# Row-paired transposes of the rows and of the attention output through the output's PSUM bank, and xT ahead of weighting

## The chip, the core and the metric

The kernel runs on one core of a Trainium2 chip. A core has TensorE (PE in the profile; PEld is its loading of weights), VectorE (DVE), ScalarE (ACT), GpSimd (POOL) and SyncE (SP, which here only starts transfers). PSUM, where TensorE writes, has eight banks. The metric is the device time in microseconds of one execution, as the median over several runs; lower is better.

## What is computed

Four layers follow one another: attention with a memory, a gated feed-forward layer, and both once more, each with a layer norm in front and a residual addition behind. Cut to what matters, the reference is:

```python
# x: 2048 x 448; 16 heads of 256; memory of 8 rows; segments of 32 rows
for s in range(64):
    h = concatenate([mem, x[32*s:32*s+32]])        # 40 rows of 448
    q, k, v = h @ Wq, h @ Wk, h @ Wv               # for each head
    p = softmax(mask(q @ k.T * scale))             # 40 x 40 for each head
    o = sum over heads of (p @ v) @ Wo
    mem = o[:8]                                    # goes on to the next segment
    outs.append(o[8:])
...
x = x + attention(layernorm(x))
x = x + (relu(g) * u) @ W_down                     # g, u = layernorm(x) @ W_gate, @ W_up
x = x + attention(layernorm(x))                    # the same weights again
x = x + (relu(g) * u) @ W_down
```

The memory makes the segments of an attention layer a recurrence of 64 steps.

## The kernel before

**Tiling and stages.** Ahead of the loop the weights are combined: Wq with Wk to A_sb (with its last 64 input dimensions in A3 and A3z), Wv with Wo to B_sb, so that scores are (h A) h^T and outputs are sums of (p h) B. Then the loop `for g in range(nsteps + 1)` calls `step(g, ff)`. Two chains run in one step: chain 0 is the first attention layer at segment g, chain 1 the second one at segment g - 4. The steps with g below 4 or above 63 have one chain. The 40 rows of each chain lie transposed in `hT` (dimensions on partitions, four chunks of 128 columns, chain 0 in columns 0 to 39, chain 1 in columns 64 to 103 of each). Every other step, from g = 3, also carries a `Feed` (ff): the residual of the attention output, layer norm, both feed-forward layers for 128 rows, and the rows for later segments. These steps are called fed here, the others bare. One more Feed closes the kernel.

**The order of work.** `mm` and `tr` hang each TensorE instruction on the one before it (`in_order`), so TensorE's order is the order of the program. The other engines' queues are ordered by the framework's planner; VectorE's and ScalarE's order may differ from the program's. Where `keep_in_program_order` stands (the layer norm, the loads ahead of the loop), the order holds there too. An engine's queue runs strictly in turn.

**PSUM.** The pool has seven banks under the tag "ps", handed out in turn, and one bank under the tag "ox", which `step` takes at its start (L592) and fills in `project_out` up to `finish`.

**One step, as far as the change touches it** (`step`, from L745):
- b0, b2: two banks of half 0's projection are opened (`open_banks`, with 64-row matmuls, two row groups side by side: the last 64 input dimensions) and closed (`close_bank`, 128-row matmuls, then copied out to TQ). A bank of index 4 (z0, z1) is copied out to TZ in two parts, one on VectorE, one on ScalarE.
- In a fed step `ff.residual()` (L404): four transposes of the attention output OT into the tile otp, and one VectorE addition to the rows `xa`; then `row_stats`.
- b1, b3, z0, z1 are opened, z0, b1, b3 closed. `hk_make` (L597) transposes the rows hT into the tile kps with four transposes; VectorE copies all of it to hk, ScalarE a second form of the last chunk. z1 is closed.
- c0, c2, c1, c3 (half 1's banks) are opened; `scores_m(0)` makes the memory's scores Sm of half 0, and VectorE and ScalarE their weights PM; c0, c2, c1, c3 are closed, with `ff.norm()` in between.
- With both chains: `flipped(PM[0])` transposes PM to pps, VectorE copies it to PT; `scores_x(0)` makes Sx; `weigh_m(0)` (L630) makes ya and yb from hk and PT, copied into Y or Z; `ff.xposed()` (L414) transposes the normed rows xn to tps and copies them to xT, once on VectorE, twice on ScalarE; then `scores_m(1)`, `scores_x(1)`, and the weights of half 0.
- `project_out(0, 0, 10)` multiplies Y or Z with B_sb into ox; the Feed's `gate_up` (ups, gps from xT) follows. `flipped_rows` (L566) transposes the later weights in pairs of row groups, into two banks ppr.

Of the kernel before, what the change touches and what calls it, by code (L numbers as in the profile page):

```python
# [8 lines left out]
BF = mybir.dt.bfloat16  # L9
F32 = mybir.dt.float32  # L10
I32 = mybir.dt.int32
AF = mybir.ActivationFunctionType
ALU = mybir.AluOpType
AX = mybir.AxisListType

DM = 448
# [5 lines left out]
L = MEM + SEG  # L22
# [9 lines left out]
HI = 128  # L32
HW = 5 * HI
W = 2 * L
# [6 lines left out]
ROWS = (slice(0, 64), slice(64, 128))  # L41
# [12 lines left out]
def build_kernel(ctx, tc, A_x, A_mem0, A_Wq, A_Wk, A_Wv, A_Wo, B_W_gate, B_W_up, B_W_down, out,  # L54
                 ntiles=16, nseg=64):
    nc = tc.nc
    P = nc.NUM_PARTITIONS
# [10 lines left out]
    psum = ctx.enter_context(tc.tile_pool(name="psum", bufs=7, space=bass.MemoryType.PSUM))  # L68
# [4 lines left out]
    def in_order(r):  # L73
        if last_pe[0] is not None:
            tc.add_manual_dep(r.ins, last_pe[0],
                              mybir.DependencyInfo(mybir.DependencyClass.NoSync,
                                                   mybir.DependencyReason.DATA),
                              reason="order of issue")
        last_pe[0] = r.ins.name

    def mm(*a, **k):
        in_order(nc.tensor.matmul(*a, **k))  # L82

    def tr(*a):
        in_order(nc.tensor.transpose(*a))  # L85

    def evac(eng, dst, src):
        if eng is nc.scalar:
            nc.scalar.copy(dst, src)  # L89
        else:  # L90
            eng.tensor_copy(dst, src)  # L91
# [10 lines left out]
    ident = glob.tile([P, P], BF, name="ident")  # L102
# [50 lines left out]
    for hf in range(2):  # L153
        t = glob.tile([P, 5, 6, 64], BF, name=f"TQ{hf}")
        nc.gpsimd.memset(t[:], 0.0)
        TQ.append(t)

    def row_stats(t):

        stats = p_ln.tile([P, nc.vector.BN_STATS_DIM], F32, tag="ln_stats")  # L160
        nc.vector.bn_stats(stats[:], t[:])
        mv = p_ln.tile([P, 2], F32, tag="ln_mv")
        nc.vector.bn_aggr(mv[:], stats[:])
        rstd = p_ln.tile([P, 1], F32, tag="ln_rstd")
        nc.gpsimd.tensor_scalar(out=rstd[:], in0=mv[:, 1:2], scalar1=EPS, scalar2=None, op0=ALU.add)
        nc.gpsimd.tensor_tensor(out=rstd[:], in0=rstd[:], in1=half[:], op=ALU.pow)
        return t, mv, rstd
# [213 lines left out]
    OT = main.tile([P, 4, 128], BF, name="OT")  # L381
# [11 lines left out]
    class Feed:  # L393
# [8 lines left out]
            self.nx = xp[i % 2]  # L402

        def residual(self):  # L404
            tp = psum.tile([P, 4, 128], BF, tag="ps", name="otp")
            for kd in range(4):
                tr(tp[:, kd, :], OT[:, kd, :], ident[:])
            nc.vector.tensor_tensor(self.x[:], tp[:].rearrange("p k d -> p (k d)")[:, 0:DM], self.x[:], op=ALU.add)
            self.st = row_stats(self.x)

        def norm(self):
# [54 lines left out]
    def moving(hb, j, idx, chains, rows=slice(0, P)):  # L466

        if len(chains) == 2:
            return hb[rows, j, idx * HI:(idx + 1) * HI].rearrange("p (c k) -> p c k", k=64)[:, :, 0:L]
        c = chains[0]  # L470
        return hb[rows, j, idx * HI + 64 * c:idx * HI + 64 * c + L]
# [34 lines left out]
    def close_bank(bk, chains, hb, j, eng):  # L506

        n = L * len(chains)
        hf, N = bk.hf, len(bk.tiles)
        for t in bk.tiles:  # L510
            for kd in range(3):
                mm(bk.out(t, n), A_sb[:, kd, hf, t, :], moving(hb, j, kd, chains), start=False, stop=(kd == 2),
                   skip_group_check=True)
        ps = bk.ps
        if bk.i < 4:
            at = 2 * (bk.i // 2) + bk.i % 2
            parts = [(eng, slice(0, P), TQ[hf][:].rearrange("p g (k b) w -> p g k (b w)", b=2)[:, :, :, 32 * at:32 * at + 32], 3)]
        else:
            parts = [(nc.vector, slice(0, 64), TZ[hf][0:64, :, 0:64].unsqueeze(2), 1),
                     (nc.scalar, slice(64, 128), TZ[hf][0:64, :, 64:128].unsqueeze(2), 1)]  # L520
        for eng, rows, T, K in parts:
            T = T.rearrange("p g k (t q) -> p k t g q", q=16)
            if len(chains) == 2:
                evac(eng, T, ps[rows, 0:N * n].rearrange("p (k t g q) -> p k t g q", k=K, t=N // K, q=16))
                continue
            c = chains[0]
            src = ps[rows, 0:N * n].rearrange("p (k t w) -> p k t w", k=K, t=N // K)
            x, m = (0, SEG) if c == 0 else (MEM, 0)
            evac(eng, T[:, :, :, 2, MEM * c:MEM * c + MEM], src[:, :, :, m:m + MEM])
            evac(eng, T[:, :, :, 3 * c:3 * c + 2, :],  # L530
                 src[:, :, :, x:x + SEG].rearrange("p k t (g q) -> p k t g q", q=16))

    def queries(hf, g, kd):
        return TQ[hf][:, g, 2 * kd:2 * kd + 2, :] if kd < 3 else TZ[hf][:, g, :]
# [44 lines left out]
    def active(g):  # L579
        return [c for c in (0, 1) if 0 <= g - c * LAG < nseg]  # L580
# [3 lines left out]
    def step(g, ff):  # L584
        chains = active(g)
        xs = active(g - 1)
        ms = [c for c in chains if g - c * LAG + 1 < nseg]
        gb, j = divmod(g, BLK)
        hb = hTb[gb % 2]
        cols = [(0, 32) if c == 0 else (48, 80) for c in xs] + [(32, 40) if c == 0 else (40, 48) for c in ms]  # L590
        lo, hi = min(a for a, _ in cols), max(b for _, b in cols)
        ox = psum.tile([P, 3, W], F32, tag="ox", bufs=1, name="ox")  # L592

        def ys(hf, later=0):
            return YY[hf][(g + later) % 2]

        def hk_make():  # L597
            kps = psum.tile([P, 4, 128], BF, tag="ps", name="kps")
            for i in range(4):
                tr(kps[:, i, :], hb[:, j, i * HI:(i + 1) * HI], ident[:])  # L600
            hk = HK[g % 2]
            nc.vector.tensor_copy(hk[:, 0:4, :], kps[:])
            nc.scalar.copy(hk[:].rearrange("p k n -> p (k n)")[:, 512:768].rearrange("p (a b) -> p a b", b=64)[:, 0::3, :],
                           kps[:, 3, :].rearrange("p (a b) -> p a b", b=64))
            return hk

        def scores_m(hf):
            if not ms:
                return
            Sp = psum.tile([P, 2, L], F32, tag="ps", name="Sm")  # L610
            for kd in range(4):
                mm(Sp[:, :, :], queries(hf, 2, kd), moving(hb, j, kd + kd // 3, (0, 1)), start=(kd == 0), stop=(kd == 3))
            weights_of(Sp, 2, PM[hf], blk[:], f"m{hf}")
# [16 lines left out]
        def weigh_m(hf, hk, PT):  # L630
            if not ms:
                return
            ya = psum.tile([P, 256], F32, tag="ps", name="ya")
            for kd in range(2):
                mm(ya[:, kd * 128:kd * 128 + 128], hk[:, kd, :], PT[:], start=True, stop=True)
            nc.vector.tensor_copy(ys(hf)[:, 0:16, M0:M0 + 16], ya[:].rearrange("p (t q) -> p t q", q=16))  # L636
            yb = psum.tile([P, 192], F32, tag="ps", name="yb")
            mm(yb[:, 0:128], hk[:, 2, :], PT[:], start=True, stop=True)
            for eo in range(2):
                mm(yb[:, 128:192], hk[:, 4 + eo, :], PT[:, 64 * eo:64 * eo + 64], start=(eo == 0), stop=(eo == 1))  # L640
            nc.scalar.copy(ys(hf)[:, 16:28, M0:M0 + 16], yb[:].rearrange("p (t q) -> p t q", q=16))
# [46 lines left out]

        def project_out(hf, t0, t1):

            for t in range(t0, t1):
                for mc in range(3):
                    mm(ox[:, mc, lo:hi], B_sb[:, hf, t, mc * 128:(mc + 1) * 128],
                       ys(hf)[:, t, lo:hi], start=(hf == 0 and t == 0 and mc == 0),
                       stop=(hf == 1 and t == NT - 1 and mc == 2), skip_group_check=True)
# [56 lines left out]
        b1, b3, z0, z1 = open_banks(chains, hb, j, (0, 1), (0, 3), (0, 4), (1, 4))  # L752
        close_bank(z0, chains, hb, j, None)
        load_some()
        close_bank(b1, chains, hb, j, nc.vector)
        close_bank(b3, chains, hb, j, nc.scalar)
        hk = hk_make()
        close_bank(z1, chains, hb, j, None)
        c0, c2, c1, c3 = open_banks(chains, hb, j, (1, 0), (1, 2), (1, 1), (1, 3))
        scores_m(0)  # L760
        close_bank(c0, chains, hb, j, nc.scalar)
# [5 lines left out]
        if len(chains) == 2:  # L767
            pm = flipped(PM[0], 1, "m0")
            Sx0 = scores_x(0)
            weigh_m(0, hk, pm)  # L770
            if ff is not None:
                ff.xposed()
            scores_m(1)
            Sx1 = scores_x(1)
            probs_x(0, Sx0)
        else:
            Sx0 = scores_x(0)
            if ff is not None:
                ff.xposed()
            scores_m(1)  # L780
            Sx1 = scores_x(1)
            pm = flipped(PM[0], 1, "m0")
            weigh_m(0, hk, pm)
            probs_x(0, Sx0)
# [27 lines left out]
        pm = flipped(PM[1], 1, "m1")  # L812
# [17 lines left out]
    for g in range(nsteps + 1):  # L830
        if g == LAG - 1:
            set_mem(LAG, mem0T[:].unsqueeze(2), (1,))
        i = (g - 3) // 2
# [68 lines left out]
```

## Time and profile before

| what | value |
|---|---|
| runs | 1599.98, 1600.96, 1604.62 us; median 1600.96 |
| the profiled execution | 1600.11 us, of which the span is 1598.3 us |
| mean granted clock of TensorE | 0.993 |
| chain that ended last | PE 89%, DVE 7%, ACT 1%, POOL 1%, issue 1% |
| steps with transposes kps / otp | 68 x 4 / 34 x 4 transposes |
| hk on VectorE / on ScalarE | 68 x 424 ns / 68 x 266 ns |
| residual addition on VectorE | 34 x 381 ns |
| xT on VectorE / on ScalarE | 34 x 421 ns / 68 x 473 ns |
| DMA in the loop | about 10 GB/s |

In lines of a timeline the columns are the start and the duration in us, the engine, the line of the program, the operation, out<-in by tile names, the shapes, and the number of instructions merged into the line. A matmul's duration in the records is its latency, some 0.2 us; the next one starts long before it ends, so the pace of TensorE is read from the distances between starts. In 40 slices of the span, TensorE is busy at 0.9 and more from the sixth slice on, VectorE at 0.7, ScalarE at 0.4 to 0.5.

### The profile page before, as it was taken

To read this page: it belongs to the slowest core of one execution; us is meant where nothing else is said; L and a number is where in the kernel's file an instruction comes from. 1 tells how busy PE (TensorE), PEld (TensorE's weight loads), DVE (VectorE), ACT (ScalarE), POOL (GpSimd) and SP (SyncE) were. 2 spreads that over 40 slices of the span, in tenths; PEclk is the share of its full clock that TensorE was granted. 3 is DMA by queue.
4 is the path that set the end of the run, shared out by engine and by line. 5 is a ranking of instruction groups with operands and counts; after the bars stand their busy time and mean duration, and the time that the engine had idled before them with its cause. 6 is when DMAs were issued, how large, how long until landed. Compare 5 with 4: busy or idle time off the path is not lost.

```text
span 1598.3 us, 96401 instructions
## 1 busy us (share of the span) xinstructions
PE 1567.8 (98%) x44356; PEld 1439.8 (90%) x44356; DVE 1142.5 (71%) x3859; ACT 762.9 (48%) x2239; POOL 92.9 (6%) x240
## 2 busy tenths in 40 slices
PE   8989999999999999999999999999999999999997
PEld 7678899999999999999999999999999999999886
DVE  6856777777777777777777777777777777777773
ACT  5634445544444445544444445544444445544432
POOL 2110000000000000000000000000000000000000
PEclk9989999999999999999999999999999999999999
DMA  9530000000000000000000000000000000000000
GB/s 257 147 102 8 9 9 4 10 9 10 10 10 9 10 10 4 10 10 9 10 10 10 10 10 4 10 10 10 10 9 9 10 10 4 10 8 7 7 7 6
DMA packets 29461, 33.01 MB, mean 21 GB/s; under 512 B 3320, under 2 KB 28160, under 8 KB 29056
## 3 DMA queue, kind: packets, MB, share of 16 engines
q1 hardware_dynamic: 28992, 26.85, 6.3%
q8 instruction: 346, 5.67, 1.5%
q14 instruction: 59, 0.48, 0.1%
q0 software_dynamic: 64, 0.01, 0.0%
HBM read 23.18 MB, written 1.84 MB: 16 GB/s over the span
## 4 chain that ended last, share of the span: by engine, by line
PE 89%; DVE 7%; ACT 1%; POOL 1%; issue 1%; DMA 0%; POOLq 0%; ACTq 0%; DVEq 0%
PE prj L82 25%; PE ox L82 25%; PE ups L82 10%; PE dps L82 6%; PE o L82 5%; PE y L82 4%; PE Sx L82 2%; PE Sm L82 2%; PE bps L82 1%; PE tpw L85 1%; DVE xn L175 1%; DVE TQ L91 1%; PE aps L82 1%; PE gps L82 1%; PE tps L85 1%; PE pps L85 1%
## 5 line engine op out<-in xcount | busy, mean ns | idle before, releaser
L82 PEld LDWEIGHTS <-B_sb 128*128 128x128 bf16 (+1 forms) x15456 | 495.0, 103 | 27.7 <-issue 19.9
L82 PE MATMUL prj<-hT,A_sb 128*128 128x80 bf16 (+1 forms) x11424 | 441.7, 200 | 0.4 <-issue 0.4
L82 PEld LDWEIGHTS <-A_sb 128*128 128x128 bf16 x11424 | 411.9, 100 | 8.9 <-issue 0.5
L82 PE MATMUL ox<-Y,B_sb 128*128 128x80 bf16 (+4 forms) x5880 | 223.0, 198 | 1.8 <-DVE Y L636 1.8
L82 PE MATMUL ox<-Z,B_sb 128*128 128x80 bf16 (+2 forms) x5712 | 217.7, 199 | 1.3 <-DVE Z L636 1.3
L89 ACT CAST TQ<-prj 128x480 bf16<-128x480 f32 (+1 forms) x380 | 178.5, 497 | 83.0 <-PE prj L82 58.7
L82 PE MATMUL gps<-xT,Wgu_sb 64*128 64x128 bf16 (+1 forms) x3332 | 191.3, 214 | 0.8 <-issue 0.5
L82 PE MATMUL ups<-xT,Wgu_sb 64*128 64x128 bf16 (+1 forms) x3332 | 191.1, 214 | 1.0 <-DVE xT L416 0.5
L82 PEld LDWEIGHTS <-Wgu_sb 64*128 64x128 bf16 x6664 | 179.4, 95 | 4.8 <-issue 2.5
L91 DVE CAST TQ<-prj 128x480 bf16<-128x480 f32 (+1 forms) x228 | 129.3, 573 | 13.4 <-PE prj L82 11.2
L432 DVE SCALAR_TENSOR_TENSOR hh<-gps,ut 128x256 bf16<-128x256 f32 (+1 forms) x238 | 95.3, 407 | 48.0 <-ACT ut L431 35.3
L431 ACT CAST ut<-ups 128x256 bf16<-128x256 f32 (+1 forms) x238 | 85.4, 359 | 83.4 <-PE gps L82 64.9
L91 DVE CAST Y<-y 64x128 bf16<-64x128 f32 (+2 forms) x256 | 102.2, 420 | 14.4 <-ACT Y L89 4.5
L89 ACT CAST Y<-y 64x128 bf16<-64x128 f32 (+2 forms) x256 | 89.4, 379 | 46.6 <-DVE Y L91 41.5
L91 DVE CAST Z<-y 64x128 bf16<-64x128 f32 (+2 forms) x256 | 99.2, 418 | 12.4 <-ACT Z L89 5.5
L89 ACT COPY hT<-tps 128x256 bf16<-128x256 bf16 x32 | 11.9, 372 | 197.5 <-DVE hT L91 197.5
L563 DVE COPY PT<-pps 128x128 bf16<-128x128 bf16 (+1 forms) x206 | 49.6, 254 | 79.1 <-PE pps L85 77.5
L545 ACT ACTIVATE se<-se 128x80 f32<-128x80 f32 (+1 forms) x270 | 71.4, 298 | 68.0 <-DVE se L544 67.2
L89 ACT CAST TZ<-prj 64x320 bf16<-64x320 f32 (+2 forms) x152 | 56.2, 380 | 98.8 <-DVE TZ L91 94.0
L89 ACT CAST Z<-y 64x128 bf16<-64x128 f32 (+2 forms) x256 | 89.2, 378 | 23.9 <-DVE Z L91 17.4
L82 PEld LDWEIGHTS <-hk 40*128 40x128 bf16 (+1 forms) x1989 | 79.9, 95 | 20.5 <-issue 10.6
L551 DVE TENSOR_REDUCE ssum<-se 128x2 f32<-128x80 f32 (+1 forms) x270 | 70.8, 274 | 35.9 <-ACT se L545 33.6
(128 smaller groups left out, 2254.6 us busy)
## 6 DMA issues: line engine op xcount, KB each, us to landing
wo<-in_A_Wo_dram SPq DMA_DIRECT2D x8, 448.0 KB, 7.6
nat<-in_A_Wq_dram SPq DMA_DIRECT2D x8, 384.0 KB, 5.5
nat<-in_A_Wk_dram SPq DMA_DIRECT2D x8, 384.0 KB, 6.1
nat<-in_A_Wv_dram SPq DMA_DIRECT2D x8, 384.0 KB, 7.6
xa<-in_A_x_dram SPq DMA_DIRECT2D x32, 56.0 KB, 2.4
xa<-xp SPq DMA_DIRECT2D x32, 56.0 KB, 1.9
out_dram<-xa SPq DMA_DIRECT2D x32, 56.0 KB, 2.0
xp<-in_A_x_dram SPq DMA_DIRECT2D x30, 56.0 KB, 2.3
```

The source lines that it names most:

```text
L82: in_order(nc.tensor.matmul(*a, **k))
L85: in_order(nc.tensor.transpose(*a))
L89: nc.scalar.copy(dst, src)
L91: eng.tensor_copy(dst, src)
L175: nc.vector.tensor_scalar(out=xn[:, o:o + b - a], in0=t[:, a:b], scalar1=mv[:, 0:1], scalar2=rstd[:], op0=ALU.subtract, op1=ALU.mult))
L431: nc.scalar.copy(ut[:, :, n], ups[:, :, n])
L432: nc.vector.scalar_tensor_tensor(out=hh[:, 2 * u:2 * u + 2, n], in0=gps[:, :, n], scalar=0.0, in1=ut[:, :, n], op0=ALU.max, op1=ALU.mult)
L545: nc.scalar.activation(se[:], se[:], AF.Exp, scale=SCALE)
L551: nc.vector.tensor_reduce(ssum[:], se[:], axis=AX.X, op=ALU.add)
L563: nc.vector.tensor_copy(PT[:], pps[:].rearrange("p b q -> p (b q)"))
```

## The change

A new helper `flipped_dims` makes eight transposes of 64 rows in place of four of 128: for each chunk one of dimensions 0 to 63 and one of dimensions 64 to 127, in two row groups of the array, into two PSUM tiles. The first tile takes the bank "ox", the second one a bank "ps". It serves `residual` and `hk_make`. The residual's addition becomes two, over the 64-column groups with even and with odd number (4 and 3 of them). hk is copied out by VectorE (first half) and ScalarE (second half, and the form of the last chunk, now read with a broadcast). Sm of half 0 takes the bank "ox" too, and the tile ox is taken only at the first `project_out`. In the order, `hk_make` goes behind the closing of z1, and, with both chains, `ff.xposed()` ahead of `weigh_m(0)`.

```diff
+    def flipped_dims(name, src):
+
+        two = [psum.tile([P, 4, 64], BF, name=name, **where) for where in (dict(tag="ox", bufs=1), dict(tag="ps"))]
+        for kd in range(4):
+            for r in range(2):
+                tr(two[r][:, kd, :], src(r, kd), ident[ROWS[r], ROWS[r]])
+        return two
...
         def residual(self):
-            tp = psum.tile([P, 4, 128], BF, tag="ps", name="otp")
-            for kd in range(4):
-                tr(tp[:, kd, :], OT[:, kd, :], ident[:])
-            nc.vector.tensor_tensor(self.x[:], tp[:].rearrange("p k d -> p (k d)")[:, 0:DM], self.x[:], op=ALU.add)
+            tp = flipped_dims("otp", lambda r, kd: OT[ROWS[r], kd, :])
+            xd = self.x[:].rearrange("p (c d) -> p c d", d=64)
+            for r in range(2):
+                nc.vector.tensor_tensor(xd[:, r::2, :], tp[r][:, 0:4 - r, :], xd[:, r::2, :], op=ALU.add)
             self.st = row_stats(self.x)
...
-        ox = psum.tile([P, 3, W], F32, tag="ox", bufs=1, name="ox")
+        ox = None
...
         def hk_make():
-            kps = psum.tile([P, 4, 128], BF, tag="ps", name="kps")
-            for i in range(4):
-                tr(kps[:, i, :], hb[:, j, i * HI:(i + 1) * HI], ident[:])
+            kps = flipped_dims("kps", lambda r, kd: hb[ROWS[r], j, kd * HI:kd * HI + HI])
             hk = HK[g % 2]
-            nc.vector.tensor_copy(hk[:, 0:4, :], kps[:])
+            for r, eng in enumerate((nc.vector, nc.scalar)):
+                evac(eng, hk[:, 0:4, 64 * r:64 * r + 64], kps[r][:])
             nc.scalar.copy(hk[:].rearrange("p k n -> p (k n)")[:, 512:768].rearrange("p (a b) -> p a b", b=64)[:, 0::3, :],
-                           kps[:, 3, :].rearrange("p (a b) -> p a b", b=64))
+                           kps[1][:, 3, :].unsqueeze(1).to_broadcast([P, 2, 64]))
...
-            Sp = psum.tile([P, 2, L], F32, tag="ps", name="Sm")
+            Sp = psum.tile([P, 2, L], F32, name="Sm", **(dict(tag="ps") if hf else dict(tag="ox", bufs=1)))
...
+            nonlocal ox
+            if ox is None:
+                ox = psum.tile([P, 3, W], F32, tag="ox", bufs=1, name="ox")
...
+        close_bank(z1, chains, hb, j, None)
         hk = hk_make()
-        close_bank(z1, chains, hb, j, None)
         c0, c2, c1, c3 = open_banks(chains, hb, j, (1, 0), (1, 2), (1, 1), (1, 3))
         scores_m(0)
...
             Sx0 = scores_x(0)
-            weigh_m(0, hk, pm)
             if ff is not None:
                 ff.xposed()
+            weigh_m(0, hk, pm)
             scores_m(1)
```

## The prediction

> **What bounds the kernel.** I read the page first, then the timeline of two neighbouring steps in the middle (one with the feed-forward half, called fed, one without, called bare), then the groups by form for durations.
>
> ```profile
> PE 1567.8 (98%) x44356; PEld 1439.8 (90%) x44356; DVE 1142.5 (71%) x3859; ACT 762.9 (48%) x2239; POOL 92.9 (6%) x240
> ```
>
> TensorE is busy 98% of the span and is 89% of the chain that ended last. Its order is fixed by hand, so time is won only by taking TensorE work out, and lost wherever the next matmul in that order must wait. The busy share hides short waits, because a matmul lasts some 0.2 us in the records while the next starts 0.036 us later; so I go by distances between starts. The kernel repeats itself: a fed and a bare step together take 44.95 us (kps starts at 755.38, 782.06, 800.33 in the trace).
>
> **The stretch around the transposes of the rows, a fed step.** TensorE, then VectorE:
>
> ```profile
> 800.33 0.39 PE L85 MATMUL kps<-ident,hT 128*128 128x128 bf16 x4
> 800.56 0.59 PE L82 MATMUL prj<-hT,A_sb 128*128 128x80 bf16 x12
> 801.08 0.60 PE L82 MATMUL prj<-hT,A 64*128 64x80 bf16 x24
> 801.62 0.28 PE L82 MATMUL Sm<-hT,TQ 128*128 128x80 bf16 x3
> ```
> ```profile
> 800.03 0.64 DVE L91 CAST TQ<-prj 128x480 bf16<-128x480 f32 x1
> 800.76 0.42 DVE L602 COPY hk<-kps 128x512 bf16<-128x512 bf16 x1
> 801.19 0.48 DVE L91 CAST TZ<-prj 64x320 bf16<-64x320 f32 x1
> 801.97 0.24 DVE L542 TENSOR_REDUCE mx<-Sm 128x2 f32<-128x80 f32 x1 [0.30 <-PE Sm L82]
> ```
>
> The reader is to see four distances: 4 transposes 0.23 us (0.056 each); z1's 12 matmuls 0.39 (11 distances of 0.036) and then 0.13 to the first 64-row matmul, a change from whole-array to row-paired work; the 24 row-paired matmuls with the change back, 0.54. From kps to Sm it is 1.29 us, in the bare step too (827.01 to 828.30). VectorE is idle for 0.30 us just ahead of mx.
>
> **Part 1: the paired transposes.** The trace has the same form already, in flipped_rows:
>
> ```profile
> 809.57 0.19 PE L85 MATMUL ppr<-ident,PM 64*128 64x64 bf16 x2
> 809.60 0.22 PE L85 MATMUL ppr<-ident,PX 64*128 64x64 bf16 x4
> 809.66 0.22 PE L82 MATMUL ups<-xT,Wgu_sb 64*128 64x128 bf16 x1
> ```
>
> Six transposes, three pairs, take 0.09 us: 0.03 a pair. Four pairs take 0.12 in place of 0.23, a gain of 0.11 us a set. Between 64-row matmuls they pay no change (ups follows at once). The diff puts hk_make straight in front of the row-paired opening of the c banks, so the change of 0.13 that stood there now stands in front of the transposes, and none is added. [...]
>
> The attention output's set:
>
> ```profile
> 797.82 0.39 PE L85 MATMUL otp<-ident,OT 128*128 128x128 bf16 x4
> 798.14 0.39 PE L82 MATMUL prj<-hT,A 64*128 64x80 bf16 x12
> ```
>
> 0.32 us, that is 4 x 0.056 and 0.10 of change. After, the change comes ahead of the set and row-paired matmuls follow: again 0.11 less. The residual becomes two VectorE additions. 448 elements take 0.38; copies of 128, 256 and 512 elements take 0.22, 0.29 and 0.42, so 256 and 192 come to about 0.28 and 0.25, of which 0.08 overlaps (below): 0.07 later on VectorE. Behind it wait row_stats, TZ of z0 and TQ of b1; TQ ends at about 800.74 in place of 800.67, still ahead of z1's end (800.81), so it is covered. Uncovered it would cost 0.07 in 33 steps, 2.3 us. Sum of this part: 33 x -0.11 = **-3.6 us**.
>
> **Part 2: the shared bank, where the gain of hk goes.** The first half of kps, then Sm of half 0, then ox use one bank in turn. So Sm's first matmul now waits for the copy of that half, on VectorE. That copy stands behind TZ of z1 on VectorE: z1 is earlier both in the program and on TensorE. I count from the start of z1, T. TensorE alone: 0.39 + 0.13 + 0.12 + 0.54 = 1.18 to Sm. VectorE: z1's last matmul starts at 0.39 and lasts 0.20; TZ follows 0.04 later (as mx follows Sm) and takes 0.48; the copy of 128x256 takes 0.28 and starts 0.08 before TZ ends (the group PT<-pps of that size: 288 ns; where both are ready, VectorE's instructions overlap by 0.08: TZ at 799.66 lasts 0.45, TQ starts at 800.03); TensorE starts 0.055 after the copy (PT ends at 805.00, ya starts at 805.06). Together 0.39 + 0.20 + 0.04 + 0.48 - 0.08 + 0.28 + 0.055 = 1.365. So Sm would wait 0.185 us, and comes 1.365 after T, against 1.29 before (kps's start is then T): +0.075 a step in place of -0.11. The wait stalls TensorE itself: behind Sm in its queue stand 72 matmuls of the c banks, and with them every later operation. What hangs on Sm (max, exp, PM) keeps its distance to it; PM is ready 0.55 us before its transpose (803.80 to 804.35). ACT takes the other half of hk (0.37, as hT<-tps of that size), which nobody awaits before ya. 67 steps x 0.075 = **+5.0 us**. Bounds for a step: -0.11 (the copy goes ahead of TZ), +0.155 (no overlap). I take the middle, since the nearest pair of rows (TZ then TQ) overlaps. That half 0's scores leave the other seven banks frees one there; no matmul waits for one in these steps, so it is worth nothing.
>
> **Part 3: xT in front of weighting (30 fed steps with both chains).**
>
> ```profile
> 804.79 0.18 PE L82 MATMUL Sx<-hT,TZ 128*128 128x40 bf16 x1
> 805.06 0.27 PE L82 MATMUL ya<-PT,hk 128*128 128x128 bf16 x2
> 805.17 0.28 PE L82 MATMUL yb<-PT,hk 128*128 128x128 bf16 x3
> 805.28 0.39 PE L85 MATMUL tps<-ident,xn 128*128 128x128 bf16 x4
> ```
> ```profile
> 804.79 0.21 DVE L563 COPY PT<-pps 128x128 bf16<-128x128 bf16 x1
> 805.00 0.32 DVE L542 TENSOR_REDUCE mx<-Sx 128x4 f32<-128x160 f32 x1
> 805.37 0.42 DVE L636 CAST Z<-ya 128x256 bf16<-128x256 f32 x1
> 805.71 0.42 DVE L416 COPY xT<-tps 128x512 bf16<-128x512 bf16 x1
> ```
>
> Sx's last matmul to ya is 0.27 us, where 0.025 would do: ya waits for PT. The four transposes (4 x 0.056 = 0.22) fit into that wait, and ya still starts at 805.06. So the first matmul of ox, at 806.05 before, could start at 805.83. But ox reads what Z<-ya writes (TensorE's waits name it: ox waited 7 times for Y or Z of L636, 3.1 us, in steps where weighting stands directly ahead of it), and xT's copy now reaches VectorE ahead of it: mx ends at 805.33, xT runs 805.25 to 805.67, Z 805.58 to 806.01, ox starts at 806.06. The 0.22 gained at ya is lost at ox: 30 x +0.01 = **+0.3 us**. If VectorE takes Z first, ox starts at 805.84: -0.21 a step, -6.2 us. xT's two ACT copies move forward too (to about 805.8, behind Z<-yb); ups, at 807.2, then has more room. No DMA moves, and SP and POOL see nothing of the change. The 8 steps with one chain keep their order here; the closing feed stands alone at the end and I count it as nothing, within 0.1 us.
>
> **Sum:** -3.6 + 5.0 + 0.3 = +1.7 us on the profiled execution's 1600.11 us (span 1598.3): 1601.8. That execution lies 0.85 under the median of the runs shown (1600.96), so on the median it is 1602.7; between the two I say **1602.3 us**. That is no change that can be told: a measurement of this kernel tells about 0.3% from nothing, 4.8 us.
>
> **Rivals.**
> The copy of hk's first half goes ahead of TZ on VectorE. For it: the planner sets VectorE's order, and mx<-Sx already runs ahead of Z<-ya against the program's order. Against: that happened because ya was not finished, and here z1 is finished first. The full gain then stands: 67 x -0.11 - 3.6 + 0.3 = -10.7 us, 1590 on the median. Chance 0.16.
> Z<-ya goes ahead of xT, the rest as forecast: 1.4 - 6.2 = -4.8 us, 1596, at the edge of what can be told. Chance 0.08, half of it counted as faster.
> Slower: hk's copy does not start under the tail of TZ, or its four runs of 64 cost 0.08 more than the plain copy. Sm is then 0.155 a step later, 67 x 0.155 = 10.4, with -3.6 + 0.3 = +7.1 us, 1608. It decides from 0.125 a step on (8.4 - 3.6 + 0.3 = 5.1 us). For it: copies that wait for ACT on a bank run without overlap (Z at 797.28 and 797.58). Against: PT at 804.79 starts 0.08 before TQ ends. Chance 0.20.
> The two transposes of a pair don't run side by side when fed from hT and OT: the gain of otp is gone, 1.7 + 3.6 = +5.3 us, 1606; for hk the wait of 0.185 covers the 0.12 more. Against: ppr. Chance 0.06, also slower.
> The forecast keeps 0.50.
>
> **From cases to numbers.** Faster by over 0.3%: 0.16 + 0.04 = 0.20. Slower: 0.20 + 0.06 = 0.26. Same: 0.54. The likeliest case alone spans 1599 to 1606 (TZ took 0.45 to 0.48 us, so 0.03 a step less or more, 67 times 2 us, and the runs shown spread over 4.6). The range takes in the two outer cases: 1589 to 1610.
>
> **What would show it.** Right: kps at 0.03 a pair with 64-row prj right behind; Sm of half 0 waiting for VectorE's hk in nearly every step, near 0.19 us, with TZ directly before hk on VectorE; ya without its 0.25 us wait in fed steps, and ox waiting for Z<-ya by about 0.23. Wrong: hk ahead of TZ, no wait at Sm, or ox following Sx at once; a fed and a bare step would then take some 0.4 us less than 44.95 together.

## The result: slightly slower, for a wait that was named and one that was not

Over 20 runs each the changed kernel takes 1605.77 us (1602.46 to 1608.53) against 1602.11 us (1599.47 to 1604.62) before; the ratio is 1.0023, with a 95% interval of 1.0016 to 1.0030. The profiled execution took 1602.46 us (span 1600.7) against 1600.11. The medians are 3.7 us apart, the profiled executions 2.4: within the 0.3% that the prediction called no change, though with 20 runs each the interval lies clear of 1.

Two lines of the changed kernel's page: the busy times, and the engines' shares of the chain that ended last:

```profile
PE 1566.4 (98%) x44764; PEld 1439.2 (90%) x44764; DVE 1123.6 (70%) x3893; ACT 784.6 (49%) x2307; POOL 93.0 (6%) x240
...
PE 83%; DVE 9%; ACT 5%; issue 1%; POOL 1%; DMA 0%; ACTq 0%; POOLq 0%; DVEq 0%
```

TensorE is busy 1.4 us less, and the span is 2.4 us longer: some 4 us of waiting were added. Its share of the chain fell from 89% to 83%, what VectorE and ScalarE hold rose from 8% to 14%.

**The rows' transposes, a fed step of the changed kernel**, TensorE, then VectorE, then one line of ScalarE (start and duration in us, as in the lines of before):

```profile
801.33 0.29 PE L85 MATMUL kps<-ident,hT 64*128 64x64 bf16 x8
801.46 0.59 PE L82 MATMUL prj<-hT,A 64*128 64x80 bf16 x24
802.17 0.27 PE L82 MATMUL Sm<-hT,TQ 128*128 128x80 bf16 x3
```
```profile
800.67 0.64 DVE L91 CAST TQ<-prj 128x480 bf16<-128x480 f32 x1
801.43 0.48 DVE L91 CAST TZ<-prj 64x320 bf16<-64x320 f32 x1
801.84 0.27 DVE L91 COPY hk<-kps 128x256 bf16<-128x256 bf16 x1
802.51 0.24 DVE L550 TENSOR_REDUCE mx<-Sm 128x2 f32<-128x80 f32 x1 [0.39 <-PE Sm L82]
```
```profile
801.74 0.38 ACT L89 COPY hk<-kps 128x256 bf16<-128x256 bf16 x1
```

Eight transposes take 0.13 us to the next matmul, and that is a row-paired one with no change between. Then the last row-paired matmul and Sm are 0.315 us apart in the mean of 48 middle steps, where 0.131 stood before. VectorE shows why: TZ of z1 from 801.43, the copy of hk's first half behind it, ending at 802.11, and Sm some 0.054 later. In all 48 steps Sm starts 0.053 to 0.054 us after the end of that copy. ScalarE's copy of the second half ends at about the same time, and the page's chain runs through it in this step; but Sm starts anything from 0.042 to 0.110 us after it, so Sm follows VectorE's copy. The 0.39 us for which VectorE is idle ahead of mx are no slack: they begin when its copy lets TensorE start Sm, and mx waits for Sm.

**The attention output**, TensorE and then VectorE:

```profile
798.49 0.29 PE L85 MATMUL otp<-ident,OT 64*128 64x64 bf16 x8
798.62 0.38 PE L82 MATMUL prj<-hT,A 64*128 64x80 bf16 x12
```
```profile
799.06 0.45 DVE L416 TENSOR_TENSOR xa<-otp,xa 128x256 bf16<-128x256 bf16 x2
```

0.13 us in place of 0.32, with 0.10 paid ahead of the set. The two additions take 0.45 us together, one took 0.38.

**xT and weighting**, the same fed step, TensorE and then VectorE:

```profile
805.32 0.18 PE L82 MATMUL Sx<-hT,TZ 128*128 128x40 bf16 x1
805.35 0.38 PE L85 MATMUL tps<-ident,xn 128*128 128x128 bf16 x4
805.60 0.29 PE L82 MATMUL ya<-PT,hk 128*128 128x128 bf16 x2
...
806.36 0.18 PE L82 MATMUL Sx<-hT,TZ 128*128 128x40 bf16 x1
806.58 1.09 PE L82 MATMUL ox<-Z,B_sb 128*128 128x80 bf16 x26
```
```profile
805.33 0.22 DVE L571 COPY PT<-pps 128x128 bf16<-128x128 bf16 x1
805.54 0.33 DVE L550 TENSOR_REDUCE mx<-Sx 128x4 f32<-128x160 f32 x1
805.78 0.41 DVE L424 COPY xT<-tps 128x512 bf16<-128x512 bf16 x1
806.11 0.41 DVE L643 CAST Z<-ya 128x256 bf16<-128x256 f32 x1
```

The transposes fill the wait of ya. The wait reappears as 0.22 us between Sx and ox, because Z<-ya stands behind xT's copy on VectorE and ends at 806.52.

**What was not foreseen** is in the gate_up of the same step: the first matmul of the fourth pair of column blocks comes 0.11 us after the last transposes in the mean of 24 middle fed steps, where 0.026 stood before. TensorE, then VectorE of the kernel before (where ox starts at 806.05), then VectorE of the change (ox at 806.58):

```profile
810.13 0.22 PE L85 MATMUL ppr<-ident,PX 64*128 64x64 bf16 x4
810.27 0.21 PE L82 MATMUL ups<-xT,Wgu_sb 64*128 64x128 bf16 x1
```
```profile
806.57 0.31 DVE L542 TENSOR_REDUCE mx<-Sx 128x4 f32<-128x160 f32 x1
806.92 0.32 DVE L544 TENSOR_TENSOR se<-Sx,mx 128x160 f32<-128x160 f32 x1
807.46 0.55 DVE L551 TENSOR_REDUCE ssum<-se 128x2 f32<-128x80 f32 x2 [0.22 <-ACT se L545]
...
809.03 0.79 DVE L432 SCALAR_TENSOR_TENSOR hh<-gps,ut 128x256 bf16<-128x256 f32 x2
```
```profile
806.97 0.31 DVE L550 TENSOR_REDUCE mx<-Sx 128x4 f32<-128x160 f32 x1
807.75 0.46 DVE L559 TENSOR_REDUCE ssum<-se 128x4 f32<-128x160 f32 x2 [0.46 <-ACT se L553]
...
808.21 0.29 DVE L552 TENSOR_TENSOR se<-Sx,mx 128x160 f32<-128x160 f32 x1
...
809.55 0.32 DVE L564 TENSOR_TENSOR PX<-se,rs 128x160 bf16<-128x160 f32 x1
809.80 0.75 DVE L440 SCALAR_TENSOR_TENSOR hh<-gps,ut 128x256 bf16<-128x256 f32 x2
```

The first of the two hh instructions merged in the last line ends at 810.215 (it lasts 0.417), and ups starts 0.053 later. That hh reads a bank of the first gate_up. In all 24 steps ups starts 0.052 to 0.054 us after the end of that hh; in the kernel before it starts about 0.217 after it, so nothing waits there. The queue of VectorE is another one too: the subtraction se<-Sx,mx of half 1 stood right behind its maximum mx, ahead of the sums ssum; now it stands behind two of them, and VectorE is idle for 0.46 us ahead of the first, where it was 0.22.

### The profile page after: what moved, and what is told of

Its sections match the earlier page's. It is cut to its first block, busy times and chain, and to the rows that moved or that the text cites. A ratio compares the mean times of both kernels' runs of the same rounds, so it can differ in the third digit from the quotient of the medians.

```text
span 1600.7 us, 97370 instructions
## 1 busy us (share of the span) xinstructions
PE 1566.4 (98%) x44764; PEld 1439.2 (90%) x44764; DVE 1123.6 (70%) x3893; ACT 784.6 (49%) x2307; POOL 93.0 (6%) x240
## 4 chain that ended last, share of the span: by engine, by line
PE 83%; DVE 9%; ACT 5%; issue 1%; POOL 1%; DMA 0%; ACTq 0%; POOLq 0%; DVEq 0%
PE ox L82 25%; PE prj L82 20%; PE ups L82 8%; PE dps L82 6%; PE o L82 5%; PE y L82 3%; PE gps L82 3%; PE Sx L82 3%; PE Sm L82 2%; DVE TZ L91 2%; PE bps L82 1%; DVE TQ L91 1%; PE tpw L85 1%; ACT Z L89 1%; PE aps L82 1%
## 5 line engine op out<-in xcount | busy, mean ns | idle before, releaser
L82 PE MATMUL prj<-hT,A_sb 128*128 128x80 bf16 (+1 forms) x11424 | 430.8, 200 | 0.0
L82 PEld LDWEIGHTS <-A_sb 128*128 128x128 bf16 x11424 | 406.4, 100 | 8.4
L89 ACT CAST TQ<-prj 128x480 bf16<-128x480 f32 (+1 forms) x380 | 183.3, 494 | 82.7 <-PE prj L82 58.3
L553 ACT ACTIVATE se<-se 128x80 f32<-128x80 f32 (+1 forms) x270 | 74.7, 300 | 80.8 <-DVE se L552 58.3
L82 PE MATMUL dps<-Wd_sb,hh 128*128 128x448 bf16 x476 | 95.9, 353 | 0.0
```

The costliest lines, as they stand in the source:

```text
L553: nc.scalar.activation(se[:], se[:], AF.Exp, scale=SCALE)
```

## The experiments

Each was timed beside the kernel before on the same chip. In what follows a pair of steps is a fed and a bare step in the middle of the run, measured from one Sm of half 0 to the next (mean of 23 of each); "fed" runs from the fed step's Sm to the bare one's, so it holds the bare step's wait at Sm.

| kernel | ratio to before, 95% interval | fed, us | bare, us |
|---|---|---|---|
| before | 1 | 26.685 | 18.269 |
| the change | 1.0023 (1.0016 to 1.0030) | 26.842 | 18.226 |
| Sm in one of the seven banks | 0.9953 (0.9941 to 0.9966) | 26.670 | 18.056 |
| hk's copy ahead of TZ | 0.9959 (0.9947 to 0.9972) | 26.671 | 18.058 |
| weighting first | 1.0015 (1.0006 to 1.0024) | 26.765 | 18.227 |
| hk_make ahead of z1 | 1.0036 (1.0023 to 1.0048) | 26.882 | 18.269 |
| Sm in one of the seven, weighting first | 0.9935 (0.9921 to 0.9949) | 26.575 | 18.065 |
| Sm in one of the seven, xT's copies behind ya's | 0.9908 (0.9894 to 0.9921) | 26.432 | 18.065 |
| attention output's pairs alone | 0.9978 (0.9969 to 0.9986) | 26.681 | 18.163 |

### Sm of half 0 back in one of the seven banks

```diff
-            Sp = psum.tile([P, 2, L], F32, name="Sm", **(dict(tag="ps") if hf else dict(tag="ox", bufs=1)))
+            Sp = psum.tile([P, 2, L], F32, tag="ps", name="Sm")
```

> The change with one part undone: the memory scores Sm of half 0 take one of the seven banks again, and only the first half of kps (and of otp) shares the output's bank. Theory (Sm waits for hk's first half behind TZ on VectorE, 0.185 us in 67 steps): the wait goes, Sm follows the row-paired matmuls at 0.13 us in place of 0.316, and the time falls by 67 x 0.185 = 12.4 us against the changed kernel, to about 0.9945 of the kernel before. Rival (the eighth tile finds no free bank, because b3's copy on ScalarE is not done): the wait stays between 0.05 and 0.2 us and less than half of it is won.

The ratio is 0.9953. A fed step of this kernel on TensorE:

```profile
795.78 0.29 PE L85 MATMUL kps<-ident,hT 64*128 64x64 bf16 x8
795.91 0.59 PE L82 MATMUL prj<-hT,A 64*128 64x80 bf16 x24
796.43 0.28 PE L82 MATMUL Sm<-hT,TQ 128*128 128x80 bf16 x3
```

From kps to Sm it is 0.65 us where the changed kernel takes 0.84, and Sm follows at 0.131 us. So the eighth tile does find a bank, and the wait was that of the shared one. Sm comes 0.184 us earlier. The pair is 0.342 us shorter than with the change, 0.171 a step where 0.185 was expected; 0.010 a step is lost again between the matmuls of Sm.

### The copy of hk's first half ahead of TZ on VectorE

```diff
-        close_bank(z1, chains, hb, j, None)
-        hk = hk_make()
+        fill_bank(z1, chains, hb, j)
+        hk, first = hk_make()
+        with tc.issue_after(first):
+            empty_bank(z1, chains, hb, j, None)
```

`fill_bank` and `empty_bank` are the two halves of `close_bank`; `first` is VectorE's copy of kps's first half.

> The changed kernel with one order turned round on VectorE: the copy of hk's first half stands ahead of TZ of z1; banks and TensorE's order as in the change. Theory (it is TZ ahead of the copy that holds Sm): the copy ends 1.13 us after z1's start, Sm is held for 0.01 us at most, the time falls by about 12 us against the changed kernel, to 0.9947 of the kernel before. Rival (the shared bank costs the wait by itself, whatever the order): Sm's distance stays at 0.316 us and the time does not move.

0.9959, with the bank still shared. VectorE and then TensorE:

```profile
797.36 0.29 DVE L618 COPY hk<-kps 128x256 bf16<-128x256 bf16 x1 [0.34 <-PE kps L85]
797.57 0.47 DVE L91 CAST TZ<-prj 64x320 bf16<-64x320 f32 x1
```
```profile
797.16 0.59 PE L82 MATMUL prj<-hT,A 64*128 64x80 bf16 x24
797.71 0.27 PE L82 MATMUL Sm<-hT,TQ 128*128 128x80 bf16 x3
```

Sm follows at 0.147 us, 0.016 above its distance in a step without a wait. By itself, sharing the bank cost these 0.016 us here; what cost the 0.184 us of the change is that its reader stands second in VectorE's queue.

### Weighting ahead of xT again

```diff
-            if ff is not None:
-                ff.xposed()
             weigh_m(0, hk, pm)
+            if ff is not None:
+                ff.xposed()
```

> The changed kernel with weighting ahead of xT again in the steps with both chains. Theory (moving xT only shifts a wait from ya to ox, and its other order on VectorE and ScalarE holds the fourth pair of gate_up by 0.08 us): ya waits 0.27 us again, ox does not wait, the wait in gate_up goes, and the time falls by 30 x 0.07 = 2 us against the changed kernel, to about 1.001 of the kernel before. Rival (the move wins its 0.22 us a step): the time rises by some 6 us, to 1.006.

1.0015: the interval reaches into that of the change itself, so the two are told apart in the steps. A fed step is 0.077 us shorter than with the change (0.070 expected); ya is 0.276 us behind Sx again, ox follows Sx at once, and no wait stands in gate_up. Moving xT wins 0.018 us from Sm to ox and costs 0.08 in gate_up.

### hk_make ahead of z1 again

```diff
-        close_bank(z1, chains, hb, j, None)
         hk = hk_make()
+        close_bank(z1, chains, hb, j, None)
```

> The changed kernel with hk_make in front of the closing of z1 again, so that the paired transposes stand among whole-array matmuls, and hk's copy ahead of TZ on VectorE. Theory (each change between whole-array and row-paired work costs about 0.1 us): the set pays two changes, 0.13 + 0.12 + 0.13 us, then z1 0.39, a change 0.13 and 0.54 to Sm, in all 1.44 us where the changed kernel takes 1.366; the wait at Sm is gone, but the time rises by 67 x 0.07 = 4.7 us against the changed kernel, to 1.005 of the kernel before. Rival (paired transposes cost no change of mode): 1.18 us and a time 12 us below the changed kernel.

1.0036. A fed step on TensorE:

```profile
801.66 0.29 PE L85 MATMUL kps<-ident,hT 64*128 64x64 bf16 x8
801.88 0.60 PE L82 MATMUL prj<-hT,A_sb 128*128 128x80 bf16 x12
802.42 0.60 PE L82 MATMUL prj<-hT,A 64*128 64x80 bf16 x24
802.96 0.28 PE L82 MATMUL Sm<-hT,TQ 128*128 128x80 bf16 x3
```

The eight transposes now cost 0.22 us to z1's first matmul, as much as the four of before (0.23), and another 0.10 ahead of them. Nothing waits at Sm (0.131), and the pair is still 0.083 us longer than with the change. The sign and the mechanism hold, but 0.042 a step was measured where 0.07 was expected. The expected sum is too high in two terms: the 0.13 ahead of the set contains the 0.036 by which the whole-array matmuls ahead of it are apart, and the change back added 0.10 and not 0.13. That alone would leave almost nothing of the 0.07. Measured from the last matmul ahead of both to Sm it is 1.431 us against 1.402 with the change, 0.029 more, and 0.010 come on top between the matmuls of Sm.

### The pairs without their waits, and those of the attention output alone

Sm in one of the seven banks and weighting first, that is both edits above together:

> The paired transposes alone, with hk_make behind z1: Sm of half 0 in one of the seven banks, and weighting ahead of xT as in the kernel before. Theory (each paired set saves 0.11 us, the wait at Sm and the order of xT took it back): 67 x 0.11 + 33 x 0.11 = 11 us less than the kernel before, 0.993; 2.3 us less than the kernel with Sm in one of the seven banks and xT ahead. Rival (xT ahead of weighting carries part of the gain of that kernel): the ratio rises to 0.997.

0.9935, 10.4 us of 1601.54, where 11 were expected. A pair of steps is 44.640 us against 44.954 before, 0.314 less: three sets at 0.105. It is also 0.085 shorter than with Sm in one of the seven banks and xT ahead, 30 x 0.085 = 2.6 us where 2.3 were expected, so xT ahead carries no part of the gain.

The pairs of the attention output alone, on the kernel before (its helper, its residual, and ox taken at the first `project_out`):

> The kernel before with the paired transposes of the attention output and the two additions alone (the first tile in the output's bank, which is taken later in the step). Theory: 33 x 0.11 = 3.6 us less, 0.9977 of the kernel before; the added VectorE time of 0.07 us delays no matmul. Rival (the additions are on the path, through TZ and TQ to Sm): half of it or nothing, with a wait at Sm in the fed steps.

0.9978, 3.5 us. The bare stretch, which holds this set, is 0.106 us shorter, the other unchanged within 0.004, and Sm stands at 0.130 us in both: the second addition on VectorE delays no matmul there. Taken from the 0.314 of the kernel above, this 0.106 leaves 0.104 for each set of the rows.

### xT's transposes early, its copies behind ya's

On the kernel with Sm in one of the seven banks; `flip_rows` is the transposing half of `xposed`, `rows_out` the copying half, and `weigh_m` returns VectorE's copy of ya:

```diff
             if ff is not None:
-                ff.xposed()
-            weigh_m(0, hk, pm)
+                ff.flip_rows()
+            ya_out = weigh_m(0, hk, pm)
+            if ff is not None:
+                with tc.issue_after(ya_out):
+                    ff.rows_out()
```

> Sm of half 0 in one of the seven banks, the four transposes of xn ahead of weighting as in the change, but the copies to xT traced and queued on VectorE behind the copy of ya. Theory (the move fills the wait of ya, and only VectorE's order moves the loss to ox): ya starts 0.1 us after the last transpose at most, ox follows Sx without a wait, and a fed step is 0.15 to 0.21 us shorter than with weighting first: 30 x 0.15 to 0.21 = 4.5 to 6.2 us less than that kernel, about 0.990 of the kernel before. Rival (VectorE is behind all through this stretch, so that any time won at ya is lost at the next wait, in gate_up): less than 2 us.

0.9908, the fastest of all: 1586.34 us against 1601.54. TensorE and then VectorE of a fed step:

```profile
799.40 0.18 PE L82 MATMUL Sx<-hT,TZ 128*128 128x40 bf16 x1
799.43 0.38 PE L85 MATMUL tps<-ident,xn 128*128 128x128 bf16 x4
799.68 0.29 PE L82 MATMUL ya<-PT,hk 128*128 128x128 bf16 x2
...
800.44 0.18 PE L82 MATMUL Sx<-hT,TZ 128*128 128x40 bf16 x1
800.48 1.09 PE L82 MATMUL ox<-Z,B_sb 128*128 128x80 bf16 x26
```
```profile
800.00 0.42 DVE L650 CAST Z<-ya 128x256 bf16<-128x256 f32 x1
800.34 0.41 DVE L431 COPY xT<-tps 128x512 bf16<-128x512 bf16 x1
```

Now ya is not late and ox follows Sx after 0.04 us. Sm to ox is 0.190 us shorter than with weighting first, and 0.143 of it is left at the end of the fed stretch; the stretch from ppr to ym took 0.03 back. The median is 4.4 us below that of the kernel with Sm in one of the seven banks and weighting first (1590.76), just under the 4.5 to 6.2 expected. The rival, that all of it would be lost again, falls.

## Why the prediction was right, step by step

**The pairs.** 0.11 us a set, taken from a form that stood elsewhere in the trace, measured 0.104 (rows) and 0.106 (attention output). That the change from whole-array to row-paired work would move ahead of the set and not be added held in both places: 0.134 us ahead of each set, where 0.036 is the pace, and 0.026 behind it. The kernel with hk_make ahead of z1 pays 0.10 us for each of its changes, the one behind the set (0.123 us, where 0.026 stood) among them.

**The wait at Sm.** It was worked out as 0.185 us; the distance grew from 0.131 to 0.315, that is by 0.184. Both experiments that remove it, one by the bank and one by the order, give back 0.17 a step. This is the term that decides the sign: without it the same transposes make the kernel faster by 0.5% (0.9953) and 0.4% (0.9959).

**xT in front.** A shift of the wait from ya to ox, +0.01 us a step, was forecast; Sm to ox measured 4.419 us against 4.432, -0.013. The order of xT and Z on VectorE was the assumed one. The faster rival (Z<-ya first) did not happen, but the last experiment, which enforces it, shows that its price was right at ox, 0.19 of the 0.21, and too high for the step, of which 0.143 stays.

**What was missed.** The step said that with xT's copies earlier, "ups, at 807.2, then has more room". That looked at the first matmul of gate_up alone. The planner also laid out VectorE's later queue anew: the first hh starts 3.22 us after ox (806.58 to 809.80), where it was 2.98 (806.05 to 809.03), and the fourth gate_up waits for its bank, about 0.08 us a fed step (ppr to ym 1.730 us against 1.651), 30 x 0.08 = 2.4 us. The forecast's sum of +1.7 with these 2.4 is +4.1; the medians moved by 3.7, the profiled execution by 2.4. In a pair of steps the forecast was 2 x 0.075 - 0.11 + 0.01 = +0.05 us, and 45.068 against 44.954, that is +0.114, was measured; the wait in gate_up, 0.08, is more than the difference, and Sm to ox, 0.02 better than forecast, takes some of it back. The time of 1602.3 lies 3.5 below the 1605.77 measured: 1.5 because it counts from 1600.6 where the kernel before took 1602.11 over 20 runs, and 2.0, the change of 3.7 less the forecast 1.7, mainly for this wait. The range, 1589 to 1610, is far wider than either and says little by itself.

Moving xT brings the wait: the kernels with weighting first lack it. Among the traces it goes with the order on VectorE. The change and the three experiments with xT in front that have half 1's subtraction behind the two sums wait in every one of the 24 steps (0.10 to 0.12 us to ups in the mean); the kernel before and the three experiments with weighting first have the old order and no wait. The last experiment has the old order too, with xT's transposes ahead, and 0.061 us to ups. That order alone was never changed, so that it is what makes hh late is not shown, and why the planner chose it stays open.

**The rivals.** hk's copy ahead of TZ did not happen. Made to happen, it gives 0.9959, that is 6.6 us less than before where the rival was priced at 10.7; the wait in gate_up, which its price did not hold, is 2.4 of the difference. The slower one, no overlap behind TZ, fell: the copy starts at 801.84 while TZ lasts to 801.92. That the pairs would not run side by side from hT and OT fell with the 0.13 us per set of eight.

## What to carry to other kernels

When a tile moves into a bank that others use in turn, the cost was here not the bank (0.016 us a step) but the place of its last reader in the reader's queue (0.184): follow that queue up to the first instruction that will now wait. Idle time on an engine said nothing here about how fast it answers, since the idle time itself waited for the engine that asks: VectorE's 0.30 us ahead of mx did not keep Sm from waiting 0.184. And moving work into a wait won here only when the copies that it brings did not stand ahead of the ones that are due next (0.143 us a fed step; with the copies ahead, 0.077 was lost); split the move, with the TensorE part early and the copies behind.

## What the runs showed of the hardware beyond what was expected

Two VectorE instructions on different tiles and of different sizes, both with their inputs ready, overlapped here by 0.07 to 0.08 us: TZ of 64 rows ends 0.073 to 0.076 us after the copy of 128 rows behind it has started, in 48 steps of the changed kernel.

A change between whole-array and row-paired work added the same 0.10 us in the three places measured, counted from one start to the next: 0.134 us from whole-array matmuls into the pairs, where 0.036 is the pace; 0.131 from row-paired matmuls of 80 columns to Sm, where 0.033 is the pace from pair to pair; and 0.123 from row-paired transposes to z1's matmuls in the kernel with hk_make ahead of z1, where 0.026 leads on to row-paired matmuls.
